# v's square three steps later in ScalarE's order, block 0's sums copied by two engines, and the survey's tiles laid last

## The chip, the cores and the metric

The kernel runs on one core of one Trainium2 chip. The metric is the device time of one execution in microseconds (us). Five engines work side by side, each through its own list in order: TensorE (PE: matmuls and transposes; PEld its weight loads), VectorE (DVE), ScalarE (ACT), GpSimd (POOL), and SyncE (SP), which here issues all DMAs. They wait for each other through semaphores. SBUF has 128 partitions; a tile's size is given in bytes per partition. PSUM holds what TensorE sums.

## The reference, cut to what matters

Three stages follow each other; the output of one is the input of the next.

```python
# 1. attention with decay: B, H, S, D = 4, 8, 576, 64
scores = scale * q @ k.T + (cum[:, :, :, None] - cum[:, :, None, :])   # causal; cum: running sum of log f
x = softmax(scores) @ v                                                # as 2304 rows of 512
# 2. MLP with cosine: 512 -> 2048 -> 512
h = x @ w_in
x = (h * cos(h)) @ w_out
# 3. mixture of 8 experts, 512 -> 1024 -> 512, all experts on all rows
P = exp(x @ w_gate - max); 8 times: rows to sum 1, columns to sum 1, times N / E
out = sum over e of P[:, e] * (relu(x @ w1[e]) @ w2[e])
```

## The kernel before, in words

All matmuls of 2. and 3. take their operands as two fp16 halves, a high and a low part ("splits"), with scales that are powers of two found from sums or maxima of the data. The order of every engine is the order in which the code issues instructions.

**Attention** goes through 16 pairs of heads, seven steps each (`PS`), so step `7 n` is the first of pair `n`. In each step x, `on_pe`, `on_act`, `on_dve` and `go("pool", x)` issue the engines' parts: scores three steps ahead, row limits two, exponentials one, transposes (`turn`, L660) and the weighted sums of v (`weigh`, L710) one step behind. The preparation of a pair is put at steps before it by the table `PREP`: (engine, step relative to `7 n`), the second entry for pair 0. `v_sq` is `square_v` (L474), on ScalarE: the sum of squares of v, read from `vraw`, which SP loads by DMA 12 steps before the pair (`ld`). `v_sum` is `scale_v`: a matmul with ones into PSUM (L132), one VectorE operation (L137) and three GpSimd operations (L142 to L146) that make v's scale. `sp0`, `sp1`, `sp2` are the three GpSimd operations of `split_v` (L464, L466, L468). `ACT_ORDER` sets in what order a step's exponentials (E), high parts (H) and prepared work (X) come on ScalarE. Between these, `pieces` reads and splits the MLP's first weights, and `split_row` (L227, L164, L165) splits the attention's output.

**The MLP** runs over items (block b of hidden tiles, chunk j of rows, tile i): `BLOCKS` 3, 4, 5, 4 tiles of 128 hidden columns, chunks of 384, 384, 512, 512, 512 rows. `layer1` (L264), `between` (L283 to L291: the cosine on ScalarE and VectorE), `layer2` (L956) two items later, into four PSUM banks, one for each 128 output columns x. After a chunk's last tile `finish` takes the four banks out: in block 0 ScalarE copies with a factor (L970), in later blocks VectorE adds (L972). Weights sit in nine slots `w0` to `w8`; unit u uses slot u mod 9, so `w7` and `w8` serve only units 7 and 8 of block 2 (`w3` to `w6` serve block 3 too). Beside the MLP, `survey` (L906) reads all expert weights once on ScalarE through two tiles `seen0` and `seen1`, 64 chunks, one per item, to find their scales. In block 3 `split_x` copies each finished chunk into `XL[j % 2]` (L989, L990), `logits` (L1004) multiplies it with the gate's weights, and keeps the result in a part of `seen` (`lg`, L1008) for `logits2` (L1018). `scale_first` (L1085) scales rows 0 to 767 of x in two pairs.

**The experts** begin behind `mctx.close()`. The pool `xp` is laid over the bytes of `big`, `early`, `late` and `bc`, with waits tile by tile. GpSimd first runs `prepare_alone(0)` (scale L1223, sums L1246, high parts L1273, low parts L1286; into `wa00`), `prepare_alone(1)` (into `wa01`), `prepare_alone(2)` (`wb00`), `combine_first` (L1306, L1307, L1310: seven combinations of rows 0 to 767 into `xc`), `prepare_alone(3)` (`wb01`), in this order; then what is hooked into the products. "Job" below is such a number. The 48 groups that follow each take a first layer (14 products of 6 matmuls of 384 columns, L1465) and a second layer (7 times 18 matmuls of 256 columns, L1586). Low parts of h come from GpSimd (L1494, L1500) and VectorE.

**Where the tiles lie.** A pool's tiles lie in the order of the code. Counted in bytes per partition from the start of `big`, which is that of `xp` too, `bc` begins at 75,200:

```text
bc:  seen0 75,200  seen1 79,296  w3..w6 83,392  XL[0] 99,776  XL[1] 116,160
     tmw1 132,544  tmw2 136,640  w7 140,736  w8 144,832  end 148,928
xp:  wa00 16,384  wb01 23,552  ...  wb10 112,640  wb11 119,808  st 126,976
     wa01 130,048  wb00 137,216  end 144,384
```

The pool `bc` as a whole waits for attention's pools, which lie at the same bytes; `xc` of the first group lies in `keep2`, elsewhere.

Of the kernel before, what the change touches and what calls it, by code (L numbers as in the profile page):

```python
# [11 lines left out]
F32 = mybir.dt.float32  # L12
# [5 lines left out]
ALU = mybir.AluOpType  # L18
# [5 lines left out]
def kernel(  # L24
# [13 lines left out]
    nc = tc.nc  # L38
    P = 128
    B, NH, S, D = q.shape  # L40
    NT, DM = out.shape
# [29 lines left out]
    def unit(b, i):  # L71
        return sum(BLOCKS[:b]) + i
# [173 lines left out]
    def at(where, n, fn):  # L246
        where.setdefault(n, []).append(fn)
# [9 lines left out]
    def layer1(b, j, i):  # L257
        n = CH[j][1]
        w = W[unit(b, i) % NSLOT]
        ps = ps_h.tile([P, 512], F32, tag="h", name="ph")  # L260
        first = True
        for kk in range(KD):
            for ws, xs in PASSES:
                nc.tensor.matmul(  # L264
                    ps[:, 0:n],
                    w[:, ws, kk * P : (kk + 1) * P],
                    XT[j][:, xs, kk, :],
                    start=first,
                    stop=kk == KD - 1 and (ws, xs) == PASSES[-1],
                )  # L270
                first = False
        return ps
# [21 lines left out]
    with tc.manual_schedule():  # L294

        with ExitStack() as actx:
# [204 lines left out]
            def lo_in(n, which, h):  # L501
# [32 lines left out]
                "dk0": (("pool", -5), ("dve", -4)),  # L534
                "ql0": (("dve", -7), ("dve", -4)),
                "kl0": (("pool", -5), ("dve", -4)),
                "sp0": (("pool", -3), ("pool", -2)),
                "sp1": (("pool", -2), ("pool", -2)),
                "ql1": (("dve", -5), ("dve", -2)),
                "sp2": (("pool", -2), ("pool", -2)),  # L540
                "v_sq": (("act", -8), ("act", -3)),
                "v_sum": (("pool", -6), ("pool", -3)),
                "ld": (("pool", 2), ("pool", 2)),
                "x_act": (("act", 11), ("act", 11)),
                "dq0": (("dma", -7), ("pool", -4)),
# [319 lines left out]
        bc = mctx.enter_context(tc.tile_pool(name="bc", bufs=1))  # L865
# [2 lines left out]
        totals = ps_c.tile([P, 512], F32, name="totals")  # L868
        spare_bank[0] = lambda: totals
        late_[0] = True  # L870
        seen = [bc.tile([P, 2 * DM], F32, name=f"seen{i}") for i in range(2)]
        LASTU = {u % NSLOT for u in range(unit(NB1 - 1, 0), NUM)}
        for s in range(NWA, NSLOT):
            if s in LASTU:
# [3 lines left out]
        for s in range(NWA, NSLOT):  # L878
            if s not in LASTU:
                W[s] = bc.tile([P, 2, 2 * DM], F16, name=f"w{s}")  # L880
        small = {}
        for nm, w in (("rs", NT // P), ("cs", NE), ("cf", NE), ("gm", 1), ("gr", 1), ("ngm", 1)):
            small[nm] = keep.tile([P, w], F32, name=nm)
# [80 lines left out]
        def finish(b, j, step):  # L964
            c0, n = CH[j]
            for x, ps in enumerate(a_of.pop((b, j))):
                a = acc[:, x, c0 : c0 + n]
                sc = down[:, b, j : j + 1]
                if b == 0:
                    nc.scalar.activation(a, ps[:, 0:n], AF.Copy, scale=sc)  # L970
                else:
                    nc.vector.scalar_tensor_tensor(a, ps[:, 0:n], sc, a, ALU.mult, ALU.add)  # L972
            if b == NB1 - 1 and j < NCH - 1:
                xl = XL[j % 2][:, :, :, 0:n]
                splits = split_x(j, xl)
                for x in range(KD):
                    if j < 2:
                        next(splits)
                    else:
                        at(after_l2, step + x // 2, lambda: next(splits))  # L980

                when = step + (5 if j == 1 else 3)
                at(after_l1, when, lambda: logits(j, xl, when, bank_h))

        def split_x(j, xt):
            c0, n = CH[j]
            for x in range(KD):
                a = acc[:, x, c0 : c0 + n]
                nc.scalar.copy(xt[:, 0, x, :], a)  # L989
                nc.vector.tensor_tensor(xt[:, 1, x, :], a, f32(xt[:, 0, x, :]), ALU.subtract)  # L990
                nc.vector.tensor_reduce(
                    largest[:, KD * j + x : KD * j + x + 1], a, axis=AX.X, op=ALU.max, apply_absolute_value=True
                )
                yield
# [4 lines left out]
        def logits(j, xt, step, bank):  # L999
            n = CH[j][1]  # L1000
            ps = bank()
            for kk in range(KD):
                for s in range(2):
                    nc.tensor.matmul(  # L1004
                        ps[:, 0:n], wg_of[0][:, kk, :], xt[:, s, kk, :], start=kk + s == 0, stop=kk == KD - 1 and s == 1
                    )
            lg = seen[j % 2][:, 0:512]
            nc.scalar.copy(lg[0:16, 0:n], ps[0:16, 0:n])  # L1008
            if step is not None:
                at(after_l2, step, lambda: logits2(j, lg, bank))  # L1010
            return lg

        def logits2(j, lg, bank):
            c0, n = CH[j]
            ps = bank()
            nt = n // P
            for x in range(nt):
                nc.tensor.matmul(  # L1018
                    ps[:, x * NE : (x + 1) * NE], lg[0:16, x * P : (x + 1) * P], sel, start=True, stop=True
                )  # L1020
            nc.vector.tensor_copy(
                gate[:, c0 // P : c0 // P + nt, :], ps[:, 0 : nt * NE].rearrange("p (t e) -> p t e", e=NE)
            )
# [66 lines left out]
        for n in range(len(items) + LAG):  # L1090
            if n in (1, 3, 5, 7):
                split_row(NCH - 1, n // 2)
            if n < len(items):
                ps = ahead.pop(n) if n in ahead else layer1(*items[n])
            for fn in after_l1.pop(n, []):
                fn()
            if n >= LAG:
                b, j, i = items[n - LAG]
                layer2(b, j, i)
                if i == tiles_of(b) - 1:  # L1100
                    finish(b, j, n)
            if n < len(items) and items[n] not in H_of:
                between(*items[n], ps)
            now[0] = n
            if n < 9 or n % 2:
                next(pieces, None)
            for fn in after_l2.pop(n, []):
                fn()
# [253 lines left out]
        def bank(kind):  # L1362
            return ps_e.tile([P, 512], F32, tag=kind, name=kind, bufs=3 if kind == "y" else 5)
# [309 lines left out]
        for blk, (e, hb) in enumerate(blocks):  # L1673
# [4 lines left out]
            for idx, p in enumerate(order):  # L1678
                base = blk * NB + idx * NS
                if (e, hb) == (1, 0):  # L1680
                    for x in range(TT):
                        a = acc[:, :, (p * TT + x) * P : (p * TT + x + 1) * P]
# [38 lines left out]
```

## Time and profile before

| | us |
|---|---|
| median of 3 runs (2056.05 to 2058.11) | 2058.07 |
| the profiled execution | 2055.7 |
| its span, from first to last instruction | 2054.0 |
| TensorE busy in it | 1953.0 (95%) |
| VectorE | 1474.0 (72%) |
| ScalarE | 1212.3 (59%) |
| GpSimd | 1108.3 (54%) |

Attention takes the first 270 us, the MLP goes to about 670, the experts take the rest. A timeline row reads: start, duration, engine, line, operation, output<-input, shapes, count; in brackets the idle time of the engine before it and what ended it. A wait row reads: who waited for whom, us in total, how often, the longest.

### The profile page before, as it was taken

Reading aid. Unit: us, or ns where it says so; the run is one execution under the profiler, and the core shown is the slowest. Engines: PE = TensorE matmul, PEld = TensorE weight load, DVE = VectorE, ACT = ScalarE, POOL = GpSimd, SP = SyncE. Lnnn points to the kernel's source line nnn. Section 1 sums busy time; section 2 is a strip of 40 time slices with the busy share of each in tenths; the row PEclk is TensorE's granted clock in tenths of the full one; section 3 lists DMA queues with packets and bytes.
Section 4 is the critical chain, followed back from the end, with each engine's and each line's share of the span. In section 5 each row is a group of like instructions: output and inputs, shape, how many; then the busy total and the mean of one; then the engine's idle time right before and its main releaser. Section 6 shows DMA issues by size and latency. Waiting matters only on the chain.

```text
span 2054.0 us, 38769 instructions
## 1 busy us (share of the span) xinstructions
PE 1953.0 (95%) x14490; PEld 1386.2 (67%) x14490; DVE 1474.0 (72%) x3253; ACT 1212.3 (59%) x2449; POOL 1108.3 (54%) x1549
## 2 busy tenths in 40 slices
PE   6988889999999479999999999999999999999998
PEld 5777754455454257777777777777777777777776
DVE  7888867877566247888777777777777777777776
ACT  6888778767644256555555555555555555555543
POOL 6677774423030988556555555565555555655531
PEclk9999999999999689999999999999999999999999
DMA  4344335544310202220220212202202122022022
GB/s 119 87 109 100 76 124 173 176 146 144 109 44 1 85 26 75 81 85 22 78 80 25 86 32 75 85 22 76 81 25 86 32 76 85 22 76 82 14 85 63
DMA packets 133916, 157.51 MB, mean 77 GB/s; under 512 B 63840, under 2 KB 98016, under 8 KB 133728
## 3 DMA queue, kind: packets, MB, share of 16 engines
q1 hardware_dynamic: 133728, 155.03, 24.8%
q8 instruction: 114, 1.87, 0.4%
q14 instruction: 74, 0.61, 0.1%
HBM read 139.71 MB, written 10.37 MB: 73 GB/s over the span
## 4 chain that ended last, share of the span: by engine, by line
PE 80%; DVE 7%; ACT 5%; POOL 3%; DMA 2%; issue 2%; SPq 0%; ACTq 0%; DVEq 0%; POOLq 0%
PE y L1586 18%; PE y L1465 17%; PE bq L1586 14%; PE bq L1465 13%; PE ph L264 6%; PE a L956 6%; DMA vraw<-in_v_dram 2%; PE pst L660 1%; ACT E L648 1%; DVE A L680 1%; PE pv L710 1%; PE pss L603 1%; ACT t L286 1%; DVE ph L288 1%; POOL xc L1307 1%
## 5 line engine op out<-in xcount | busy, mean ns | idle before, releaser
L1586 PEld LDWEIGHTS <-h 128*128 128x128 f16 x6048 | 592.7, 98 | 87.1 <-POOL h L1500 11.0
L1465 PEld LDWEIGHTS <-wa 128*128 128x128 f16 x4032 | 395.8, 98 | 290.2 <-issue 38.5
L1465 PE MATMUL y<-xc,wa 128*128 128x384 f16 x2304 | 434.7, 328 | 26.6 <-POOL xc L1306 21.9
L1586 PE MATMUL y<-wb,h 128*128 128x256 f16 x3456 | 410.1, 273 | 10.2 <-POOL h L1500 10.2
L1500 POOL TENSOR_TENSOR h<-rt,h 128x384 f16<-128x384 f32 x192 | 175.3, 913 | 449.7 <-ACT h L1499 442.7
L1481 ACT ACTIVATE ct<-y 128x384 f32<-128x384 f32 x192 | 94.2, 490 | 447.3 <-PE y L1465 447.3
L1465 PE MATMUL bq<-xc,wa 128*128 128x384 f16 x1728 | 331.3, 328 | 1.1 <-POOL xc L1307 1.0
L1586 PE MATMUL bq<-wb,h 128*128 128x256 f16 x2592 | 308.4, 274 | 0.2 <-DVE h L1491 0.2
L1567 DVE SCALAR_TENSOR_TENSOR acc<-y,gate,acc 128x256 f32<-128x256 f32 x504 | 212.6, 478 | 48.9 <-PE y L1586 48.9
L956 PE MATMUL a<-H,w 128*128 128x512 f16 (+1 forms) x960 | 203.0, 360 | 8.0 <-ACT acc L970 3.4
L264 PE MATMUL ph<-xt,w 128*128 128x512 f16 (+1 forms) x960 | 199.8, 358 | 0.0
L1567 DVE SCALAR_TENSOR_TENSOR acc<-bq,gate,acc 128x256 f32<-128x256 f32 x378 | 159.7, 478 | 39.2 <-PE bq L1586 39.1
L956 PEld LDWEIGHTS <-w 128*128 128x128 f16 x960 | 93.6, 98 | 103.6 <-issue 12.9
L1491 DVE TENSOR_TENSOR h<-bq,h 128x384 f16<-128x384 f32 x288 | 158.2, 551 | 3.2 <-ACT h L1488 0.6
L1485 DVE SCALAR_TENSOR_TENSOR bq<-bq,ct 128x384 f32<-128x384 f32 x192 | 107.7, 561 | 68.5 <-PE bq L1465 67.7
L1485 DVE SCALAR_TENSOR_TENSOR bq<-y,ct 128x384 f32<-128x384 f32 x96 | 54.4, 566 | 140.6 <-PE y L1465 136.9
L264 PEld LDWEIGHTS <-w 128*128 128x128 f16 x960 | 93.6, 99 | 89.5
L1488 ACT CAST h<-bq 128x384 f16<-128x384 f32 x288 | 134.6, 483 | 14.2 <-DVE bq L1542 14.1
L1494 POOL TENSOR_TENSOR h<-st,h 128x384 f16<-128x384 f32 x96 | 87.9, 915 | 84.5 <-ACT h L1488 80.5
L1498 ACT ACTIVATE rt<-bq 128x384 f32<-128x384 f32 x192 | 93.7, 488 | 27.5 <-DVE bq L1485 24.8
L1246 POOL TENSOR_TENSOR tm<-sg 128x256 f32<-128x256 f32 x128 | 92.0, 730 | 15.0 <-POOL h L1494 12.3
L1499 ACT ACTIVATE h<-bq 128x384 f16<-128x384 f32 x192 | 94.4, 492 | 0.0
(268 smaller groups left out, 3236.3 us busy)
## 6 DMA issues: line engine op xcount, KB each, us to landing
xc<-xd SPq DMA_DIRECT2D x105, 384.0 KB
seen<-in_moe_w_dram SPq DMA_DIRECT2D x64, 512.0 KB
sg<-in_moe_w_dram SPq DMA_DIRECT2D x64, 512.0 KB
stg<-in_moe_w_in_dram SPq DMA_DIRECT2D x16, 512.0 KB
stg<-in_moe_w_out_dram SPq DMA_DIRECT2D x16, 512.0 KB
xd<-xc SPq DMA_DIRECT2D x14, 384.0 KB
q<-q SPq DMA_DIRECT2D x30, 160.0 KB
out_dram<-acc SPq DMA_DIRECT2D x18, 256.0 KB
```

The lines of the kernel that those rows point to most:

```text
L264: nc.tensor.matmul(ps[:, 0:n], w[:, ws, kk * P : (kk + 1) * P], XT[j][:, xs, kk, :], start=first, stop=kk == KD - 1 and (ws, xs) == PASSES ...
L956: nc.tensor.matmul(a_of[b, j][x][:, 0:n], w[:, s1, DM + x * P : DM + (x + 1) * P], H[:, s2, 0:n], start=i == 0 and n_ == 0, stop=end and n ...
L1465: nc.tensor.matmul(ps[:, 0:HN], w[:, ws, a, k, :], X[b][:, xs, k, :], start=fresh and n == 0, stop=n == 5, skip_group_check=not fresh,)
L1481: nc.scalar.activation(c, cut(ps), AF.Copy, scale=RAISE)
L1485: nc.vector.scalar_tensor_tensor(cut(c), cut(ps), RAISE, other, ALU.mult, ALU.add)
L1488: nc.scalar.copy(HT[m][c][:, 0, :], src)
L1491: nc.vector.tensor_tensor(HT[m][c][:, 1, :], src, HT[m][c][:, 0, :], ALU.subtract)
L1498: nc.scalar.activation(r, cut(ps), AF.Relu)
L1499: nc.scalar.activation(HT[m][c][:, 0, :], cut(ps), AF.Relu)
L1500: nc.gpsimd.tensor_tensor(HT[m][c][:, 1, :], r, HT[m][c][:, 0, :], ALU.subtract)
L1567: nc.vector.scalar_tensor_tensor(a, v, gate[:, tt, e : e + 1], a, ALU.mult, ALU.add)
L1586: nc.tensor.matmul(ps[:, at_ * HD : (at_ + 1) * HD], HT[m][a][:, s1, c * P : (c + 1) * P], W2T[side][m][:, s2, b, :], start=fresh and m == ...
```

## The change

In `PREP`, for all pairs but the first: v's square (`v_sq`) from eight steps ahead of its pair to five, its sum and scale (`v_sum`) from six to three, `sp0` from three to two, `sp2` from two to one. In `finish`, block 0: the copies of x = 1 and 3 go to VectorE. The two `seen` tiles are laid at the end of `bc`, so that all other tiles of `bc` lie 8,192 bytes lower, the gate's copy of x (`XL`) among them. The logits are kept in the two halves of `seen1` in place of the first halves of both tiles.

```diff
-                "sp0": (("pool", -3), ("pool", -2)),
+                "sp0": (("pool", -2), ("pool", -2)),
                 "sp1": (("pool", -2), ("pool", -2)),
                 "ql1": (("dve", -5), ("dve", -2)),
-                "sp2": (("pool", -2), ("pool", -2)),
-                "v_sq": (("act", -8), ("act", -3)),
-                "v_sum": (("pool", -6), ("pool", -3)),
+                "sp2": (("pool", -1), ("pool", -2)),
+                "v_sq": (("act", -5), ("act", -3)),
+                "v_sum": (("pool", -3), ("pool", -3)),
...
-        seen = [bc.tile([P, 2 * DM], F32, name=f"seen{i}") for i in range(2)]
         LASTU = {u % NSLOT for u in range(unit(NB1 - 1, 0), NUM)}
...
         for s in range(NWA, NSLOT):
             if s not in LASTU:
                 W[s] = bc.tile([P, 2, 2 * DM], F16, name=f"w{s}")
+        seen = [bc.tile([P, 2 * DM], F32, name=f"seen{i}") for i in range(2)]
...
-                if b == 0:
+                if b == 0 and x % 2 == 0:
                     nc.scalar.activation(a, ps[:, 0:n], AF.Copy, scale=sc)
+                elif b == 0:
+                    nc.vector.tensor_scalar(a, ps[:, 0:n], sc, None, ALU.mult)
                 else:
...
-            lg = seen[j % 2][:, 0:512]
+            lg = seen[1][:, 512 * (j % 2) : 512 * (j % 2 + 1)]
```

## Rows read from the trace of the kernel before

**Rows 1.** The page's slices: busy tenths of two engines, 40 slices of 51.35 us.
```profile
PE   6988889999999479999999999999999999999998
...
POOL 6677774423030988556555555565555555655531
```

**Rows 2.** Waits over the whole span: us in total, times, longest us.
```profile
POOL wa L1273 <- PE pl L1004: 74.5, 1, 74.5
POOL bkv L142 <- DVE bkv L137: 56.3, 16, 8.3
...
PE y L1465 <- POOL xc L1306: 21.9, 5, 10.1
PE pst L660 <- ACT E L648: 15.0, 10, 3.0
...
ACT sq L474 <- DMA vraw<-in_v_dram: 25.4, 11, 6.8
...
SPq L902 <- PE psx L740: 22.8, 1, 22.8
```

**Rows 3.** GpSimd's timeline, 565 to 742 us.
```profile
577.02 0.99 POOL L1273 TENSOR_SCALAR wa<-sg 128x512 f16<-128x512 f32 x2
...
588.05 0.72 POOL L1246 TENSOR_TENSOR tm<-sg,tm 128x256 f32<-128x256 f32 x1
663.27 0.99 POOL L1273 TENSOR_SCALAR wa<-sg 128x512 f16<-128x512 f32 x2 [74.49 <-PE pl L1004]
...
680.04 0.51 POOL L1306 TENSOR_SCALAR xc<-acc 128x384 f16<-128x384 f32 x1
...
709.73 1.12 POOL L1223 TENSOR_SCALAR sg<-sg,sw 128x1024 f32<-128x1024 f32 x1
...
720.16 1.00 POOL L1342 TENSOR_TENSOR xs<-acc 128x384 f32<-128x384 f32 x1
...
730.49 1.78 POOL L1500 TENSOR_TENSOR h<-rt,h 128x384 f16<-128x384 f32 x2
```

**Rows 4.** ScalarE's timeline, 600 to 770 us: the two pairs of scale_first.
```profile
627.06 1.76 ACT L1085 ACTIVATE acc<-acc,sx 128x768 f32<-128x768 f32 x2
...
634.57 1.76 ACT L1085 ACTIVATE acc<-acc,sx 128x768 f32<-128x768 f32 x2
```

**Rows 5.** TensorE's timeline, 636 to 760 us.
```profile
667.74 2.76 PE L956 MATMUL a<-H,w 128*128 128x512 f16 x12
...
731.46 1.67 PE L1586 MATMUL y<-wb,h 128*128 128x256 f16 x7 [7.86 <-POOL h L1500]
```

**Rows 6.** Groups by form: GpSimd 572-590, GpSimd 663-721, VectorE 588.9-662 (busy us, mean ns).
```profile
L1286 POOL TENSOR_TENSOR wa<-sg,wa 128x256 f16<-128x256 f32 x3 | 2.6, 882 | 0.0
...
L1286 POOL TENSOR_TENSOR wa<-sg,wa 128x256 f16<-128x256 f32 x3 | 1.9, 668 | 0.0
...
L990 DVE TENSOR_TENSOR xl<-acc,xl 128x512 fp32r<-128x512 f32 x8 | 5.5, 685 | 2.9 <-ACT xl L989 2.9
```

**Rows 7.** ScalarE's timeline of attention: v's square of pairs 4, 5, 10 and 11.
```profile
65.54 0.73 ACT L474 ACTIVATE sq<-vraw 128x640 bf16<-128x640 f32 x1
...
80.02 0.74 ACT L474 ACTIVATE sq<-vraw 128x640 bf16<-128x640 f32 x1
...
156.42 0.74 ACT L474 ACTIVATE sq<-vraw 128x640 bf16<-128x640 f32 x1 [1.29 <-DMA vraw<-in_v_dram]
...
173.97 0.74 ACT L474 ACTIVATE sq<-vraw 128x640 bf16<-128x640 f32 x1 [2.70 <-DMA vraw<-in_v_dram]
```

**Rows 8.** Pair 9: GpSimd's last piece of v's split; chain piece using it.
```profile
159.11 1.13 POOL L468 TENSOR_TENSOR vl<-vrest,vh 128x512 f16<-128x512 f32 x1
...
162.29 0.43 PE pv L710 x9
```

**Rows 9.** Timelines of ScalarE and VectorE, 318 to 356 us: block 0's copies.
```profile
319.57 2.40 ACT L970 ACTIVATE acc<-a,down 128x512 f32<-128x512 f32 x4
...
322.68 0.75 DVE L285 SCALAR_TENSOR_TENSOR t<-ph,turnv,t 128x512 f32<-128x512 f32 x1 [3.79 <-ACT t L283]
```

## The prediction

> **What bounds the kernel now.** I read the page's slices first, then the waits, then the timelines of the stretch that stood out. In the slices [rows 1] (51.35 us each) the line of POOL is to be seen at 0 in the thirteenth (616 to 668 us) and at 9 in the next, where PE falls to 4: GpSimd does nothing, and then everything waits for it. The waits [rows 2] name the cause. GpSimd's largest single wait is 74.5 us, in front of the first write of a `wa` tile, for the matmul of L1004 that reads the copy of x in `xl`. TensorE afterwards waits 21.9 us for GpSimd's `xc`. GpSimd's timeline [rows 3] gives the order: job 1 (`prepare_alone(1)`) stops at 588.8, goes on at 663.3, combine_first starts at 680.0, job 3 at 709.7, the hooked work at 720.2. TensorE [rows 5] ends the MLP at 670.5, then starves; its stream is whole again at 731.5. From there on it is at 9 tenths in every slice but the last [rows 1], so what is won before 731 is won at the end.
>
> The second thing in the waits is in attention: ScalarE waited 11 times, 25.4 us in all, for v's DMA in front of v's square (L474), and TensorE 15.0 us for the exponentials (L648) that stand behind it in ScalarE's order. Attention is bound by no one engine; its steps hang on each other.
>
> **Part 1: the tiles.** By sizes, before, `XL[1]` covers bytes 116,160 to 132,544 (from the start of `big`) and the last stage's `wa01` bytes 130,048 to 137,216: 2,496 bytes are shared, and so job 1's first write waited for the last reader of `XL[1]`. With `seen` last, `XL[1]` ends 8,192 bytes lower, at 124,352. `wa01` then lies over `tmw2`, `w7` and `w8`; `wb00` (137,216 to 144,384) over `w8` and `seen0`. `w7` and `w8` are done with at the end of block 2, `tmw2` with the last unit, `seen0` with the survey; all that is over before 588. `seen1`, which still holds the gate's logits, lies above 144,384, under no tile of the last stage; hence the new place of `lg`. So the 74.5 us wait goes.
>
> What is late next? GpSimd runs the rest of job 1 and job 2 from 588.8, 16.8 us long (680.04 - 663.27), done by 606 to 611 with TensorE and VectorE in their MLP work. Then combine_first needs `scale_first` (L1085), done for rows 0 and 1 at 628.8 and for rows 2 and 3 at 636.3 [rows 4]. Its length is 29.7 us (709.73 - 680.04); a tenth of it (B11) fits in front of 636.3, the other 26.7 run from there to 663.0. Job 3 takes 10.4 (720.16 - 709.73): 673.4 if nothing slows it. The point that stood at 720.2 thus comes 46.8 us earlier.
>
> This work ran almost alone before; now it lies beside VectorE's MLP tail. The row for that price: the same low half of `wa` takes 882 ns beside VectorE and 668 without it [rows 6], a third more, but only there; the other operations of job 0 are as fast as later. VectorE has 8 subtractions with both inputs in SBUF (L990) in the way, 5.5 us in all [rows 6]. Bounds: 0 to 5.5 us on GpSimd; I take 2, since only the operations of that one line showed a stretch, and 1 us for the MLP itself (bounds 0 to 3, half the L990). The Trainium skill, SBUF — State Buffer, "Who interferes with whom", speaks against the change here: a VectorE instruction with two SBUF inputs and a GpSimd instruction that reads SBUF exclude each other, and one waits the whole instruction. By that rule the 5.5 us would be lost in full, and the sum would be 3.5 us smaller; the 882 ns row bears it out in kind.
>
> Job 3 then ends at 675.4, 44.8 us earlier. TensorE has its first layer, 14 products of 6 matmuls of 384 columns, from 670.5 to about 684.5 (2.76 us for 12 of 512 columns [rows 5] makes 0.17 for one, 14.5 for 84; less, since that row's last end overhangs). The second layer waited for GpSimd's lows (L1500), 11.3 us after job 3 [rows 3, 5]: 686.7 in place of 731.5, again 44.8. If GpSimd doesn't decide, TensorE does, at 684.5: 47. Minus 1 for the MLP: **44 us, bounds 38 (both contentions at their upper end) to 47**.
>
> That `seen` is last costs nothing at the survey's start: SP's wait of 22.8 us for its first load ended with the last reader in attention's pools (L740) [rows 2]; `bc` waits for those pools as a whole, so the place within it is no matter.
>
> **Part 2: v's square.** ACT's square, TensorE's column sum, VectorE's one and GpSimd's three small operations (`scale_v`) move three steps; split_v's first and third piece move one. No DMA moves, and SP's order stays. A step is 2.1 us (14.5 us a pair by seven), so the square stands 6.3 us later. The waits are one of 6.8 at the second pair, four of 2.6 to 3.2 and six small ones, so the DMA has landed at every pair but perhaps the second. A pair without a wait takes 14.5 us (65.54 to 80.02); the four with 2.6 to 3.2 us of wait take 17.5 to 18.1, as 156.42 to 173.97 [rows 7]. Taking the four to 14.6 gives 4 x 3.0 = 12 us. The six small ones (25.4 - 6.8 - 11.4 = 7.2 us) stand in pairs that are no longer than the others and give 0 to 3; the first gives 0 to 2, its start being bound by the first loads. Sum 12 to 17 if nothing takes their place.
>
> What is late next is GpSimd: its three operations now stand between the k parts and v's split. Pair 9's split ended at 160.2, and TensorE used it at 162.3 [rows 8]: 2 us of room, the least of the pairs read. The three cost 0.8 us, and split_v's last piece comes behind one step's other work. So it fits, barely, and in some pairs GpSimd will now end last. Bounds for the part: 3 to 18; I take **13**, near the four long pairs, which rest on two rows that agree.
>
> **Part 3: the copies of block 0.** Ten of 20 copies (2.40 us for four on ScalarE) go to VectorE, which stands idle 3.8 us at that place, waiting for ScalarE's next activation [rows 9]. That comes 1.2 us earlier. But TensorE is full through this block. 0 to 2; I take **1**; VectorE's idle time hides the new work, and without that cover it would cost 1.3 us a chunk, 6.5 in all.
>
> **Sum.** 44 + 13 + 1 = 58 us. The profiled execution took 2055.7 us (span 2054.0), 2.4 below the median of the runs, 2058.07. I set it against the median, rounding down for that: **1999 us**.
>
> **Rivals.** (A) Part 1 comes, part 2 doesn't: GpSimd's split of v takes the place of the DMA as what attention waits for. For it: the 2 us of room at pair 9. Against: GpSimd stood waiting in front of its three operations for 56.3 us in 16 pairs [rows 2], which it can now use. 2058 - 45 = 2013, 2007 to 2017.
> (B) The layout doesn't free job 1: another tile under `wa01` or `wb00`, or the copy of x in `xc`, holds GpSimd until the MLP's end at 671. Then combine_first starts at 671 to 680: 2058 - 14 - (0 to 9) = 2035 to 2044, by its middle 2040. Against it: job 0 wrote `wa00`, over `w1` and `w2`, at 577.0 without a wait while the MLP ran [rows 3], so tiles are waited for one by one.
> (C) Slower: v's split comes so late that TensorE's first weighted sums of each pair wait for it. The place is L710 at a pair's second step; to eat the 45 us of parts 1 and 3 it must be over 3.0 us late at each of 15 pairs. If the whole delay of 6.3 us reaches the split, less the 2 of room, it is 15 x 4.3 = 64 us: 2058 - 45 + 64 = 2077, 2062 to 2080. Against it: the split itself moves one step, 2.1 us, and only the k parts and 0.8 us stand in front of it.
>
> **How the numbers follow.** Forecast 0.68 (its own range 1987 to 2008), A 0.17, B 0.10, C 0.03, between B and no change 0.02. Low end: 47 + 18 + 2 = 67, 1991, less the 2.4 us of the profiled execution and some for pairs that gain more, 1985. The high end takes A in and a little of B's side: 2022. B and C stay out, 0.15 with the no change between. Faster by over 0.2% (4 us, what a measurement of this kernel can tell from no change): 0.95; within it 0.02; slower 0.03.
>
> **What would show it.** GpSimd's row for L1273 with no wait near 589; combine_first at 629 to 637; job 3's end at 673 to 679; L1586 whole from 684 to 689 with the clock at full from 640 on; no wait of L474 for `vraw` but perhaps one; pairs of 14 to 15 us throughout; `vl` (L468) not among what L710 waits for. It is wrong if a wait of tens of us stands before `wa`, `wb` or `xc` again, if TensorE's wait for L648 stays near 15 us, or if the long pairs stay at 17.5.

## The result, and the profile after

| | before | after |
|---|---|---|
| median, us | 2058.09 (2056.05 to 2058.23, 4 runs) | 1984.36 (1984.01 to 1984.58, 4 runs) |
| span of the profiled execution | 2054.0 | 1982.9 |
| first sums of block 0 taken out (start of L970) | 288.6 | 260.6 |
| first sums of block 1 taken out (VectorE) | 367.3 | 336.1 |
| last chunk of the MLP taken out (VectorE) | 668.6 | 642.8 |
| second layer of the experts whole (TensorE) | 731.5 | 661.0 |

The ratio is 0.9644, with a 95% interval of 0.9627 to 0.9661: 73.7 us faster, where 59 were forecast, and 0.6 us under the low end of the range. By the profiled executions the 71.1 us come as 28.0 in attention, 3.2 in block 0, minus 5.4 in the rest of the MLP, and 44.6 at the experts' start (731.46 - 661.01 = 70.45, less 25.8); 0.7 follow later. Lines behind L970 stand two further down than before (L990 is L992, L1085 L1087, L1586 L1588).

The page's slices after, the lines of [rows 1]:

```profile
PE   6999989999999999999999999999999999999998
...
POOL 6788875323067886454654555645556555565531
```

PE's hole of 4 tenths is gone. POOL's 0, a slice that stood at 0 before too, is GpSimd's wait for a DMA (45.8 us, to 542.0); TensorE is at 9 tenths there. The waits over the whole span, us in total, times, longest:

```profile
POOL xc L1308 <- ACT acc L1087: 21.6, 2, 16.8
...
POOL bkv L142 <- DVE bkv L137: 14.7, 8, 2.7
```

Of [rows 2], the 74.5 us in front of `wa` and all waits for `vraw` no longer occur, and GpSimd's wait for v's sum fell from 56.3 to 14.7. GpSimd's timeline after, against [rows 3]:

```profile
569.67 1.12 POOL L1225 TENSOR_SCALAR sg<-sg,sw 128x1024 f32<-128x1024 f32 x1 [5.45 <-DVE sw L925]
...
578.73 2.54 POOL L1288 TENSOR_TENSOR wb<-tm,wb 128x256 f16<-128x256 f32 x4
598.03 0.51 POOL L1308 TENSOR_SCALAR xc<-acc 128x384 f16<-128x384 f32 x1 [16.76 <-ACT acc L1087]
...
606.34 0.51 POOL L1308 TENSOR_SCALAR xc<-acc 128x384 f16<-128x384 f32 x1 [4.89 <-ACT acc L1087]
...
634.71 1.55 POOL L1225 TENSOR_SCALAR sg<-sg,sw 128x1024 f32<-128x1024 f32 x1
...
647.65 1.00 POOL L1344 TENSOR_TENSOR xs<-acc 128x384 f32<-128x384 f32 x1 [1.72 <-ACT acc L1332]
```

Jobs 1 and 2 run through to 581.3. The combinations wait for the scaled rows of x alone (16.8 and 4.9 us), as the prediction had it, and job 3 starts at 634.7. TensorE, against [rows 5]:

```profile
641.92 2.76 PE L956 MATMUL a<-H,w 128*128 128x512 f16 x12
644.52 1.14 PE L1467 MATMUL y<-xc,wa 128*128 128x384 f16 x6
...
661.01 0.94 PE L1588 MATMUL y<-wb,h 128*128 128x256 f16 x7 [0.94 <-POOL h L1502]
```

The first layer follows the MLP at once, and the second has one wait of 0.94 us left where [rows 5] had 7.86 and, ahead of it, the waits for `xc`.

Attention: `e<-pss,maskt` (VectorE, L642) stands once in each pair, at the same step. Before, pairs 9 to 10:

```profile
168.60 0.75 DVE L642 CUSTOM_DVE_ANT_0 e<-pss,maskt 128x576 f32<-128x576 f32 x1
...
186.78 0.75 DVE L642 CUSTOM_DVE_ANT_0 e<-pss,maskt 128x576 f32<-128x576 f32 x1
```

After, the same pairs and one more:

```profile
152.96 0.75 DVE L642 CUSTOM_DVE_ANT_0 e<-pss,maskt 128x576 f32<-128x576 f32 x1
...
166.37 0.75 DVE L642 CUSTOM_DVE_ANT_0 e<-pss,maskt 128x576 f32<-128x576 f32 x1
...
179.44 0.75 DVE L642 CUSTOM_DVE_ANT_0 e<-pss,maskt 128x576 f32<-128x576 f32 x1
```

The long pair went from 18.2 us to 13.4, the next is 13.1. The granted clock in such a stretch, before (the whole, and two microseconds of it) and then after (busy us and count of PE, PEld, DVE, ACT, POOL; clock; DMA share; GB/s):

```profile
41.00:59.00 18.00, 14.51 (x146) 12.70 (x146) 13.56 (x41) 12.75 (x26) 8.89 (x12) 0.91 0.52 123
54.00:56.00 2.00, 2.00 (x15) 1.88 (x14) 1.87 (x8) 1.57 (x3) 0.00 (x0) 0.50 0.37 82
```

```profile
41.00:59.00 18.00, 16.02 (x186) 14.30 (x187) 16.83 (x57) 15.41 (x32) 10.58 (x16) 1.00 0.55 120
```

In each of the four long pairs of before, TensorE ran for some microseconds at the lower of its two levels (0.50, that is 1.2 in place of 2.4 GHz), after having stood still behind ScalarE's wait, as here:

```profile
51.92 0.84 PE L660 MATMUL pst<-ident,E 128*128 128x128 f32 x3 [2.44 <-ACT E L648]
```

After, the clock is 1.00 in all stretches of attention that were read. So what a long pair lost was the wait and the slower matmuls behind it.

### The profile page after: what moved, and what is told of

It reads as the page before. It is cut to its first block, busy times and chain, and to the rows that moved or that the text cites. A ratio compares the mean times of both kernels' runs of the same rounds, so it can differ in the third digit from the quotient of the medians.

```text
span 1982.9 us, 38801 instructions
## 1 busy us (share of the span) xinstructions
PE 1925.6 (97%) x14490; PEld 1371.4 (69%) x14490; DVE 1481.5 (75%) x3263; ACT 1207.2 (61%) x2439; POOL 1112.9 (56%) x1549
## 4 chain that ended last, share of the span: by engine, by line
PE 81%; DVE 9%; ACT 6%; POOL 2%; issue 2%; DVEq 0%; ACTq 0%; POOLq 0%
PE y L1588 19%; PE y L1467 18%; PE bq L1588 14%; PE bq L1467 14%; PE a L956 7%; PE ph L264 6%; DVE A L680 1%; ACT E L648 1%; ACT A L672 1%; DVE ph L288 1%; PE pst L660 1%; ACT t L286 1%; DVE acc L974 1%; DVE xl L992 1%; DVE t L285 1%
## 5 line engine op out<-in xcount | busy, mean ns | idle before, releaser
L1588 PEld LDWEIGHTS <-h 128*128 128x128 f16 x6048 | 590.6, 98 | 77.0 <-POOL h L1502 1.2
L1588 PE MATMUL y<-wb,h 128*128 128x256 f16 x3456 | 408.9, 273 | 0.9 <-POOL h L1502 0.9
L1588 PE MATMUL bq<-wb,h 128*128 128x256 f16 x2592 | 306.7, 273 | 0.2 <-DVE h L1493 0.2
L956 PEld LDWEIGHTS <-w 128*128 128x128 f16 x960 | 93.3, 98 | 102.7 <-issue 12.6
L1500 ACT ACTIVATE rt<-bq 128x384 f32<-128x384 f32 x192 | 93.7, 488 | 21.5 <-DVE bq L1487 18.8
```

The costliest lines, as they stand in the source:

```text
L956: nc.tensor.matmul(a_of[b, j][x][:, 0:n], w[:, s1, DM + x * P : DM + (x + 1) * P], H[:, s2, 0:n], start=i == 0 and n_ == 0, stop=end and n ...
L1500: nc.scalar.activation(r, cut(ps), AF.Relu)
L1588: nc.tensor.matmul(ps[:, at_ * HD : (at_ + 1) * HD], HT[m][a][:, s1, c * P : (c + 1) * P], W2T[side][m][:, s2, b, :], start=fresh and m == ...
```

## The experiments: each part alone

Times "under" before are differences of medians from runs on the same chip, unless a profile is named. Times "over" the changed kernel go by its 1984.36 of the first table; beside the later experiments it had 1983.45 (changed_again), so they are good to about 1 us at best.

**tiles_only**: the kernel before with the tiles' places and the logits' alone.

```diff
-        seen = [bc.tile([P, 2 * DM], F32, name=f"seen{i}") for i in range(2)]
...
                 W[s] = bc.tile([P, 2, 2 * DM], F16, name=f"w{s}")
+        seen = [bc.tile([P, 2 * DM], F32, name=f"seen{i}") for i in range(2)]
...
-            lg = seen[j % 2][:, 0:512]
+            lg = seen[1][:, 512 * (j % 2) : 512 * (j % 2 + 1)]
```

> The kernel before with the tiles' new places and the logits in seen1 alone; PREP and block 0's copies stay. Theory by the two traces: 1 us on VectorE's subtractions of the gate's copy and a later stretch of the MLP's tail cost 5.4 us, GpSimd's early jobs give 44.6, so the time is 39 us under before (37 to 41), attention's start of the MLP stays at 288.6, GpSimd's job 1 has no wait, and its combinations start behind scale_first. The forecast on record had 44 (38 to 47). Rival: the MLP's tail lost its 5.4 us for block 0's and attention's sake (other phase between engines), then it is 43 to 46 under before.

Measured 2014.76 (2014.20 to 2017.57), 42.5 us under before (2057.25); the spans differ by 41.5. That is more than the 37 to 41 expected. The start of the MLP stays (288.2). The MLP's tail is longer here too, so that the loss belongs to the tiles, but by 4.1 us and not by 5.4. TensorE's stream is whole at 690.67, 40.8 us earlier:

```profile
690.67 0.94 PE L1586 MATMUL y<-wb,h 128*128 128x256 f16 x7 [0.94 <-POOL h L1500]
```

**square_only**: the kernel before with the four edits of `PREP` alone.

```diff
-                "sp0": (("pool", -3), ("pool", -2)),
+                "sp0": (("pool", -2), ("pool", -2)),
...
-                "sp2": (("pool", -2), ("pool", -2)),
-                "v_sq": (("act", -8), ("act", -3)),
-                "v_sum": (("pool", -6), ("pool", -3)),
+                "sp2": (("pool", -1), ("pool", -2)),
+                "v_sq": (("act", -5), ("act", -3)),
+                "v_sum": (("pool", -3), ("pool", -3)),
```

> The kernel before with PREP's four edits alone. Theory: attention's whole 28 us come from this part: the MLP's first copy at 260 to 261 in place of 288.6, the time 27 to 29 us under before, no wait of ScalarE for vraw. The forecast on record had 13 (3 to 18). Rival: some 10 us or more of the 28 come from elsewhere (a pool or a transfer that the tiles' places let start earlier); then this run gains 13 to 18 and the start of the MLP stays above 270.

2028.76 (2024.29 to 2030.50), 28.5 under; block 0's first copy at 262.4, 26.2 earlier. So this part's term was the one that was mis-sized.

**copies_only**: the kernel before with block 0's copies of x = 1 and 3 on VectorE alone. **copies_on_one**: the changed kernel without that.

```diff
-                if b == 0:
+                if b == 0 and x % 2 == 0:
                     nc.scalar.activation(a, ps[:, 0:n], AF.Copy, scale=sc)
+                elif b == 0:
+                    nc.vector.tensor_scalar(a, ps[:, 0:n], sc, None, ALU.mult)
```

> The kernel before with block 0's copies of x = 1 and 3 on VectorE alone. Theory: block 0 ends 3 us sooner against its start, so 3 us under before (2 to 4). The forecast on record had 1 (0 to 2). Rival: the 3.2 us that block 0 gained in the changed kernel came with the earlier attention's end (its weights and pieces of x were ready sooner); then 0 to 1.

> The changed kernel with block 0's copies all on ScalarE again. Theory: 2.4 to 3.2 us over the changed kernel (block 0 alone: 2.4 in the time, 2.7 between first copy and block 1's first sums), since the copies stand in ScalarE's order ahead of the cosine that TensorE's next products need. Forecast on record: 1 (0 to 2).

2.4 us under before (2054.88), and 2.7 over the changed kernel (1987.07). From block 0's first copy to block 1's first sums it is 78.7 us before, 76.0 in copies_only, 78.8 in copies_on_one and 75.5 in the changed kernel: 2.7 to 3.3 us. They come in small pieces. One of them, TensorE before, behind the third chunk's copies, and the same place in copies_only:

```profile
326.48 2.54 PE L956 MATMUL a<-H,w 128*128 128x512 f16 x11 [0.35 <-DVE H L291]
```

```profile
325.64 2.75 PE L956 MATMUL a<-H,w 128*128 128x512 f16 x12
```

Before, the eleven matmuls after the first wait for H, late because four copies (2.4 us) stood ahead of the cosine on ScalarE: 0.6 us with the restart. The three parts alone sum to 42.5 + 28.5 + 2.4 = 73.4 of the 73.7: they hardly touch each other.

## The experiments: what was lost in attention

Three causes were told apart: the square's wait for v's transfer in ScalarE's order (1), k's parts queued on GpSimd behind v's scale (2), the square's own 0.73 us ahead of its step's exponentials (3).

**v_first**: the kernel before, v loaded ahead of q and k, so that the square hardly waits where it stands. **sum_late**: v's sum, scale and split moved, the square not. **v_first_sum_late**: both.

```diff
-                    load_qk(n)
                     load_v(n)
+                    load_qk(n)
```

```diff
-                "sp0": (("pool", -3), ("pool", -2)),
+                "sp0": (("pool", -2), ("pool", -2)),
...
-                "sp2": (("pool", -2), ("pool", -2)),
+                "sp2": (("pool", -1), ("pool", -2)),
...
-                "v_sum": (("pool", -6), ("pool", -3)),
+                "v_sum": (("pool", -3), ("pool", -3)),
```

> The kernel before, with v's load issued ahead of q's and k's of the same pair; v's square stays eight steps ahead. It takes away (most of) ScalarE's wait for v's transfer and moves no instruction on the engines. Theory 1, the wait itself is what attention lost, with the exponentials behind it: 20 to 28 us under before, start of the MLP at 261 to 268. Theory 2, GpSimd's wait in front of v's scale with k's parts queued behind it is what was lost: 0 to 8 us. Theory 3, the square's own 0.73 us ahead of the exponentials in its step: 10 to 18 us. If q or k come too late in v's place, a new wait stands at their first use and this run decides less.

> The kernel before, with v's sum, scale and split moved as in the change, while v's square stays eight steps ahead with its wait for the transfer. Theory 1 (the square's wait in ScalarE's order is what attention lost; loading v first gave 19.7 us of the 28.5): 0 to 4 us under before, ScalarE's wait for vraw stays near 25. Theory 2 (k's parts, queued on GpSimd behind v's scale, are what was late): at least the 8.8 us that loading v first left open, 9 to 28 under before, GpSimd's 56 us wait down to 15.

> v's load ahead of q's and k's, and v's sum, scale and split moved as in the change; v's square stays eight steps ahead. Against loading v first alone (2037.6) it differs by GpSimd's (and the column sum's) place alone. Theory 2: the 8.8 us that loading v first left open against the square's move come back, 2028 to 2031. Theory 3 (the square's own 0.73 us ahead of the exponentials in its step costs them): 2034 to 2038, the long pairs stay at 15.8 us.

**square_behind_exp**: in the step of the square the exponentials and high parts go first. **behind_exp_sum_late**: that, and sum_late's edit. **square_seven**: the changed kernel with the square at -7 (`"v_sq": (("act", -7), ...`).

```diff
-            ACT_ORDER = ("XEH", "EXH", "EXH", "XHE", "XEH", "XEH", "XEH")
+            ACT_ORDER = ("XEH", "EXH", "EXH", "XHE", "XEH", "XEH", "EHX")
```

> The kernel before, with one entry of ScalarE's order changed: in the step that holds v's square the exponentials and the high parts go first, the square (with its wait for the transfer) behind them. Theory 1: the wait no longer holds the exponentials of that step, only those of the next, 2.1 us later; the four waits of 2.6 to 3.2 us fall to about 1, so 15 to 25 under before. If theory 3 holds as well, its 0.73 us come with it: 20 to 28. Theory 2: 0 to 8.

> The kernel before with the square behind the exponentials of its step (that alone: 6.2 us under before) and v's sum, scale and split moved as in the change (that alone: 3.1). If k's parts queued behind v's scale on GpSimd are what held attention once the wait for the transfer is shorter, the two together give more than their sum of 9.3: 15 to 26 under before, start of the MLP at 263 to 274. If the rest of the transfer's wait (9.3 us in 7) still holds ScalarE's own list, about their sum: 8 to 12, start at 276 to 281.

> The changed kernel with v's square at seven steps ahead in place of five: one step later than before, not three. The waits that repeat were 2.6 to 3.2 us and a step is 2.1 us, so 0.5 to 1.1 us of four waits stay if the transfers come as before. Theory: attention 1 to 6 us longer than in the changed kernel, 1986 to 1990. Rival: transfers move with the loop (they are issued by its own steps), and where pairs get shorter the landing comes later against the square; then the waits keep most of their size and it costs 8 to 18 us.

The medians, and from the profiles the start of block 0's first copy and ScalarE's wait for `vraw`:

| kernel | median, us | first copy at, us | earlier by | wait for vraw, us (times) |
|---|---|---|---|---|
| before | 2058.09 | 288.6 | | 25.4 (11) |
| sum_late | 2051.14 | 283.8 | 4.8 | 21.5 (13) |
| square_behind_exp | 2048.05 | 281.1 | 7.5 | 9.3 (7) |
| behind_exp_sum_late | 2040.18 | 276.2 | 12.4 | 8.7 (8) |
| v_first | 2037.55 | 270.2 | 18.4 | 0.8 (2) |
| square_only | 2028.76 | 262.4 | 26.2 | none |
| v_first_sum_late | 2029.23 | 261.4 | 27.2 | 3.2 (2) |
| after | 1984.36 | 260.6 | 28.0 | none |
| square_seven | 1990.56 | 269.2 | 19.4 | 3.4 (5) |

On their own chips the kernels of before had 2054.21 (sum_late, square_behind_exp, v_first_sum_late) and 2057.2 to 2058.1 (the others), so the column of the profiles is the better one to compare. It has a spread of its own: with attention as before the first copy lies at 288.2 to 291.2 in four profiles (before, tiles_only, copies_only, one_seen_last), with attention as changed at 260.6 to 262.4 in seven. So where the transfer is waited for, a difference of under 3 us tells little.

Cause 1 is worth 18.4 us by itself (19.7 by the medians, just short of the 20 to 28 expected if it were all), and cause 2 the 8.8 us between v_first and v_first_sum_late. Loading v first has a price of its own: TensorE waited 2.1 us for q's transfer in v_first and 1.5 in v_first_sum_late, in no other kernel of the table over 0.2. Cause 2 alone, sum_late, gave 4.8 us (3.1 by the medians, within the 0 to 4 of its first theory): GpSimd's wait for v's sum fell from 56.3 to 11.9 us, but GpSimd then waited for k itself, which ScalarE makes behind the square that still waited.

```profile
POOL k L560 <- ACT k L499: 33.1, 9, 5.7
```

So the two are not independent. Cause 3 fell: v_first_sum_late leaves the square ahead of the exponentials and gains as much as square_only. Cause 2 is seen on GpSimd. In v_first, near 50 us:

```profile
51.39 0.21 POOL L142 TENSOR_SCALAR bkv<-bkv 128x1 int32<-128x1 int32 x1 [6.01 <-DVE bkv L137]
...
52.23 0.67 POOL L560 TENSOR_SCALAR k<-k 64x576 fp32r<-64x576 f32 x1
```

and in the changed kernel:

```profile
43.30 0.21 POOL L142 TENSOR_SCALAR bkv<-bkv 128x1 int32<-128x1 int32 x1 [2.72 <-DVE bkv L137]
...
50.58 0.67 POOL L560 TENSOR_SCALAR k<-k 64x576 fp32r<-64x576 f32 x1 [2.88 <-ACT k L499]
```

In the first, GpSimd waits 6.0 us for v's sum, with k's copy (L560) queued behind it; k's high part had been ready on ScalarE at 50.6 (L499, 49.97 to 50.60). In the second GpSimd waits for k itself. TensorE's column sum and VectorE's one operation move together with GpSimd's three, and were not tried apart.

square_behind_exp missed its 15 to 25 us, though its wait for `vraw` fell by 16. In the trace q's high part (L497) and then the next step's exponentials now stand directly behind the square on ScalarE, and wait with it. behind_exp_sum_late doesn't decide between its two outcomes. Its first copy came 12.4 us earlier, the sum of 7.5 and 4.8, as if what is left of the transfer's wait still held ScalarE's own list. Its median was 17.0 under, against 6.2 and 3.1 for the two edits on another chip, as if GpSimd's order were the remaining brake. The profiled execution was the slowest of its four (2043.25), and the spread of the column is about 3 us. In square_seven the waits were as small as expected (the longest 1.1 us) and still cost 6.2 us by the medians and 8.6 by the profiles, beyond the 1 to 6 of the expectation. Why 3.4 us of wait cost more than themselves is open.

## The experiments: the tiles, and the MLP's tail

**one_seen_last**: the kernel before, only `seen0` last.

```diff
-        seen = [bc.tile([P, 2 * DM], F32, name=f"seen{i}") for i in range(2)]
+        seen = [None, bc.tile([P, 2 * DM], F32, name="seen1")]
...
+        seen[0] = bc.tile([P, 2 * DM], F32, name="seen0")
```

> The kernel before with seen0 alone laid last, so that the gate's copy of x lies 4,096 B lower and not 8,192; its end (128,448) is then under wa01's start (130,048). The logits stay in both. Theory (the 2,496 B that XL[1] and wa01 share are what held job 1): job 1 runs without its wait; wb00 then lies under no seen tile that is still read, and the time is that of the tiles alone, 2012 to 2017. Rival: other bytes hold GpSimd (a wait in front of wb of 25 to 50 us appears): 2035 to 2058.

2016.82 (2013.80 to 2018.37), 40.4 under; its span of 2012.1 is near that of tiles_only (2012.5), though the parts differ (its attention is 3.0 us longer, and 4.6 us are missing at the place of the last section). Neither `wa` nor `wb` is waited for. So it was the 2,496 shared bytes of `XL[1]` and `wa01`.

**logits_both**: the changed kernel with the logits in both `seen` tiles.

```diff
-            lg = seen[1][:, 512 * (j % 2) : 512 * (j % 2 + 1)]
+            lg = seen[j % 2][:, 0:512]
```

> The changed kernel, but the gate's logits kept in both seen tiles, as before. seen0 now lies under wb00, so GpSimd's job 2 has to wait until the logits of chunk 2 are read (617 in the changed kernel, where job 2 started at 569.7). Theory: job 2 starts at 616 to 619, combinations at 628, job 3 ends at 669 to 671 against 645.9, and the time is 22 to 26 us over the changed kernel (2006 to 2011). It also tells what slows the MLP's tail: GpSimd stands still from 570 to 617, so if its reads slow VectorE's subtractions of the gate's copy, the first four of 512 columns come back from a mean near 1.08 us to 0.69, and the chunk's end moves 2 us or more earlier; if the new places of the tiles do it, they stay slow.

2000.95 (2000.64 to 2001.87), 16.6 over the changed kernel, less than the 22 to 26. Job 2's scale and sums don't touch `wb00` and run at 571; only what is behind them waits, until 616.67 as expected:

```profile
POOL wb L1275 <- PE pl L1020: 40.6, 1, 40.6
```

Job 3 starts at 654.6, 19.9 us later, and TensorE's stream is whole at 676.3, 15.3 later. The run also tells what slows the MLP's tail. VectorE's subtractions for the gate's copy (two inputs in SBUF) in the changed kernel, chunk 2:

```profile
600.60 1.39 DVE L992 TENSOR_TENSOR xl<-acc,xl 128x512 fp32r<-128x512 f32 x1
...
608.91 1.39 DVE L992 TENSOR_TENSOR xl<-acc,xl 128x512 fp32r<-128x512 f32 x1
```

GpSimd beside them:

```profile
600.53 0.91 POOL L1309 TENSOR_TENSOR xc<-acc,xc 128x384 f16<-128x384 f32 x1
...
608.85 0.91 POOL L1309 TENSOR_TENSOR xc<-acc,xc 128x384 f16<-128x384 f32 x1
609.71 1.44 POOL L1312 TENSOR_TENSOR tm<-acc 128x384 f32<-128x384 f32 x1
```

and the same two subtractions in logits_both, where GpSimd stands still:

```profile
601.90 0.68 DVE L992 TENSOR_TENSOR xl<-acc,xl 128x512 fp32r<-128x512 f32 x1
...
609.41 0.68 DVE L992 TENSOR_TENSOR xl<-acc,xl 128x512 fp32r<-128x512 f32 x1
```

The first begins 0.07 us behind GpSimd's L1309, which ends at 601.44; 601.44 + 0.68 is 602.1, within 0.2 of its end at 601.99. Then GpSimd's L1312, issued at 609.71, stretches from 1.00 to 1.44 until the second subtraction has ended at 610.30. Each waits out the other's instruction. The Trainium skill, SBUF — State Buffer, "Who interferes with whom", states just this for a VectorE instruction with two SBUF inputs and a GpSimd one that reads SBUF, and the rows agree. From chunk 2's sums to chunk 3's it is 27.0 us both before and in logits_both, 28.6 in tiles_only and 30.2 in the changed kernel. In the changed kernel 1.6 of the 3.2 us are the four subtractions; the clock fell there as well, to a mean of 0.83 between 610 and 620, after TensorE had waited 2.1 us for `gate` on VectorE.

In tiles_only the 16 subtractions take 4.1 us more than before, which is the tail's whole loss there; chunk by chunk they take 0.2, 0.9, 1.6 and 1.4 us more, and the chunks are longer by as much. Its groups, and then those of 384 columns before (those of 512 are in [rows 6]):

```profile
L990 DVE TENSOR_TENSOR xl<-acc,xl 128x512 fp32r<-128x512 f32 x8 | 8.5, 1059 | 2.9 <-ACT xl L989 2.9
L990 DVE TENSOR_TENSOR xl<-acc,xl 128x384 fp32r<-128x384 f32 x8 | 5.7, 706 | 0.0
```

```profile
L990 DVE TENSOR_TENSOR xl<-acc,xl 128x384 fp32r<-128x384 f32 x8 | 4.6, 573 | 0.0
```

**job3_first**: the changed kernel with job 3 ahead of the combinations. **job3_late_scale**: that, and rows 0 to 767 scaled two steps later. **changed_again**: the changed kernel on the same chip as the latter.

```diff
         prepare_alone(2)
+        prepare_alone(3)
         combine_first()
         keep_blocks(0)
-        prepare_alone(3)
```

```diff
-            at(after_l2, 73 + x // 2, lambda x=x: scale_first(x))
+            at(after_l2, 75 + x // 2, lambda x=x: scale_first(x))
```

> The changed kernel, with job 3 of GpSimd ahead of the combinations in its order. GpSimd stood idle from 581.3 to 598.0 and again 4.9 us for the scaled rows; job 3 (11.2 us) fits in the first gap. Theory: TensorE's last wait for GpSimd there is 0.9 us, so 1 to 3 us under the changed kernel (1981 to 1983.5). Rival: job 3's weights come late or its reads meet VectorE's subtractions of the gate's copy, and the combinations start later than 598: 0 to 5 us above it.

> The changed kernel with job 3 ahead of the combinations and the scaling of rows 0 to 767 two steps later (10 us), behind the subtractions of the gate's copy of chunk 2. GpSimd then reads nothing while those run. If GpSimd's reads and the scaling in front of the copies on ScalarE are what stretched that chunk (30.2 us against 27.0), it comes back to 26 to 27.5, the four subtractions to 0.69 us, and GpSimd's combinations end at 646, in the 11.4 us that it waited; time 1980 to 1982.5, 2 to 4 under the changed kernel. Rival: the combinations now end behind the MLP, TensorE waits for xc, and the gain is lost: 1984 to 1992.

> The changed kernel once more, beside the kernel above on the same chip: 1984 to 1986, no difference beyond what two chips give.

job3_first alone gave nothing (1984.57; the expectation of 1 to 3 us missed). GpSimd's idle time only moved behind the combinations, to 11.4 us in front of L1344 at 647.4, and TensorE's last wait of 0.94 us stayed. But that room can be spent. job3_late_scale has 1980.74 (1979.31 to 1982.57, 5 runs) against 1983.45 (1983.15 to 1986.16, 4 runs), 2.7 us less and under both kernels; its ratio to before is 0.9627 [0.9614, 0.9640]. The combinations start behind chunk 2's subtractions:

```profile
610.95 0.51 POOL L1308 TENSOR_SCALAR xc<-acc 128x384 f16<-128x384 f32 x1 [18.26 <-ACT acc L1087]
```

All four subtractions are back at 0.68 us, and that chunk takes 25.95 us (618.45 - 592.50). Part of this is ScalarE's: the 1.76 us of scaling no longer stand ahead of the copies to `xl`.

## Why the prediction was right or wrong

**Part 1, right in mechanism and in its total.** 44 us (38 to 47) were forecast, 42.5 measured alone. In tiles_only the combinations start at 628.9 and, after the scaled rows 2 and 3, go on at 637.2, where 629 and 637 stood in the forecast. The contention on GpSimd came to 2.9 us for 2: the combinations took 31.8 us without their 4.9 of waiting (29.7 before) and job 3 11.2 (10.4). What it cost VectorE was set too low: 1 us with bounds 0 to 3 from "half the L990", against 4.1. The slowed GpSimd row of [rows 6] was read as a price for GpSimd above all; the same exclusion can double the VectorE instruction that comes second (0.68 to 1.39 us). The sentence on the Trainium skill's rule (5.5 us lost in full) was nearer. GpSimd then wasn't the last: TensorE was, behind the longer MLP, but for one wait of 0.94 us.

**Part 2, right in mechanism, the term mis-sized.** The step that failed is "Taking the four to 14.6 gives 4 x 3.0 = 12 us", with the 0 to 3 us for the small waits behind it. Both kinds of pair were measured from square to square [rows 7], 17.5 us the long one and 14.5 the "pair without a wait". But the square itself slides against the steps; from step to step the long pair is 18.2 and the other, before, 13.7:

```profile
63.59 0.75 DVE L642 CUSTOM_DVE_ANT_0 e<-pss,maskt 128x576 f32<-128x576 f32 x1
...
77.32 0.75 DVE L642 CUSTOM_DVE_ANT_0 e<-pss,maskt 128x576 f32<-128x576 f32 x1
```

So the difference was 4.5 us and not 3.0. Nor was 13.7 a floor: GpSimd's wait for v's sum was in it (the same pair is 13.7 in v_first and 13.1 in v_first_sum_late), and after the change such pairs take 13.1 to 13.6. The four long pairs gave 4.7 to 4.9 us each, 19.1 in place of 12. The rest, 8.9 us, came from pairs and waits that were given 1: 2.2 ahead of the first pair's step, 4.5 in the six pairs with the small waits and 2.2 in the others. Four of those six are 15.5 to 16.5 us from step to step, and so longer than the pair of 13.7, which the prediction did not see from square to square. The row that told it was in [rows 2]: 56.3 us of GpSimd's waiting, read as room that its operations could use. It was also a queue that k's parts stood in (8.8 us by v_first_sum_late). The fear that v's split would come late (the 2 us of room in [rows 8], rivals A and C) did not come true: no matmul of L710 waits for `vl`.

**Part 3**: 1 us (0 to 2) forecast, 2.4 to 3.3 measured. "TensorE is full through this block" held in the stretch that was read [rows 9], but before, TensorE waits for H twice in the block (0.35 and 0.27 us), and with the restarts it is 1.5 us behind copies_only at the block's last products. Where the rest lies was not looked for.

**Rivals and signs.** B is what logits_both brings about by another tile; its price there was 16.6 us, since only a part of one job waited. Of the signs named, three came otherwise: the second layer was whole at 690.7 in tiles_only and not by 689, for the MLP's tail; the pairs are 12.6 to 15.5 us long and not 14 to 15; and the clock was not at full throughout from 640 on (a mean of 0.66 between 740 and 745 in the changed kernel). **The range** ended at 1985, 0.6 us above the median: its low end allowed part 2 18 us.

## What to carry to other kernels

Measure a loop's period at an instruction that doesn't itself wait for what you mean to remove, and don't take the best period of before as the floor while another wait of the same loop is in it. An engine's long wait in front of a small operation is not only room; look at what is queued behind it. When an idle engine is set to work beside another, price both sides, for each instruction with two SBUF inputs on VectorE, and start it behind them if it has time.

## What the runs showed of the hardware

One VectorE instruction can be held much longer than one GpSimd instruction. In the gates' normalization of the changed kernel a product of two SBUF inputs, 0.31 to 0.57 us elsewhere, took 4.08:

```profile
735.51 4.08 DVE L1387 TENSOR_TENSOR gate<-gate,rs 128x144 f32<-128x144 f32 x1
...
744.22 0.31 DVE L1387 TENSOR_TENSOR gate<-gate,rs 128x144 f32<-128x144 f32 x1
```

while GpSimd went on without a gap:

```profile
735.56 0.67 POOL L1288 TENSOR_TENSOR wb<-tm,wb 128x256 f16<-128x256 f32 x1
736.18 0.73 POOL L1248 TENSOR_TENSOR tm<-sg,tm 128x256 f32<-128x256 f32 x1
736.87 1.30 POOL L1288 TENSOR_TENSOR wb<-tm,wb 128x256 f16<-128x256 f32 x2
738.12 1.30 POOL L1288 TENSOR_TENSOR wb<-sg,wb 128x256 f16<-128x256 f32 x2
```

Six GpSimd instructions passed before it was done. TensorE then waited 2.6 us for the sums made from it, and ran below its full clock for some us (0.66 between 740 and 745). The change did not bring this: the kernel before shows the same, 4.07 us at 808.35. In the profiles of copies_on_one, square_seven and one_seen_last the same instruction took 0.89 to 0.90 us, and the stretch from the MLP's last sums to the end was 1335.5 us in place of 1340.1. In changed_again, with the hold (4.08 us) but the clock at 1.00 behind it, it was 1338.3. So this one place moves a run by up to 4.6 us, which fits the spread of 4 to 6 us in several of these kernels; what decides it was not tried.
